# Reordering the prologue of an attention and MLP kernel: loads, transposes, column-tiled projections, and a halved last tile

## The chip, the cores and the metric

The kernel runs on one core of one Trainium2 chip. The metric is the device time of one execution in microseconds (us), the median over several runs. The profile shows one execution, whose span is about 1.8 us shorter than its measured time.

## The reference

`x` has 2048 tokens of 1024 channels. It is normalised, goes through attention with 32 heads of 32 channels, and in parallel, normalised once more, through an MLP of 3584 channels; the two are multiplied and added to `x`.

```python
xn = _layernorm(x, axis=-1)
s = attention(xn, wqkv, wo)                       # softmax(q k' / sqrt(32)) v, then @ wo
y = _layernorm(xn, axis=-1)
h = _gelu(y @ w1 + b1)
g = _silu(h @ w2 + b2)
return x + s * g
```

## The kernel before

The program is a list of operations with declared reads and writes; a small scheduler derives the semaphore waits from them. Attention is cut into 512 units (8 head groups, 8 query blocks, 8 key blocks): scores on TensorE, exponential on ScalarE, product with the values on TensorE. From unit 7 on, each unit also carries a "filler", a piece of projection, MLP or output product, so that TensorE and ScalarE are both full. Units 0 to 7 are the prologue: eight pairs of token tiles (128 tokens each) are loaded, normalised, transposed and projected to keys (K), queries (Q) and values (V), one pair per unit.

```python
load_x(0); load_x(1)
load_wq(0, (1,))              # weights of K, 512 KB
load_x(2); load_x(3)
load_wq(0, (0, 2))            # weights of Q and V
for tb in range(4, NT):
    load_x(tb)
...
def pair_kq(p):               # V likewise: 16 matmuls per pair
    for which, nm, dst, off in ((1, "KT", KT, 0), (0, "QT", QT, 256)):
        def f(e, which=which, off=off):
            for dc in range(DC):          # DC = 8
                ins = e.matmul(bank(bk, off, off + 256), lhsT=wq[:, which, dc, 0:128],
                               rhs=xnT[:, dc, t0:t0 + 256], start=dc == 0, stop=dc == DC - 1, ...)
...
def mm4(e, outs, lhs, rhs, start, stop):  # four column tiles of 32, used by every filler
    for j in range(4):
        ins = e.matmul(outs(j), lhsT=lhs(j), rhs=rhs, start=start, stop=stop,
                       tile_position=(0, 32 * j), ...)
```

Transposes of tiles 0 to 5 run on TensorE, those of tiles 6 to 15 as DMA transposes. The rule in the scheduler: a DMA names a semaphore, and waits for the previous DMA on the same one.

```python
prev = self.dlast.get(dma)
if prev is not None:
    deps.append(prev)
```

The softmax here doesn't subtract the row's maximum and nothing guards it: scores larger than these inputs give would overflow.

## Time and profile before

| | before |
|---|---|
| time, median (lowest to highest of 3) | 1092.49 us (1092.04 to 1092.57) |
| span of the profiled execution (itself 1093.07 us, 0.58 above the median) | 1091.3 us |
| scores of unit 7, of unit 8 (start) | 49.30, 51.89 us |
| TensorE matmuls in 30.35 to 49.30 | 226 |
| last full-width VectorE add of the last tile (start) | 1087.32 us |
| last store issued | 1088.89 us |

Three marks are used throughout. The start of the scores of unit 8 ends the prologue. The last full-width VectorE add marks the end of the long middle part. What follows it is the tail.

### The profile page before, as it was taken

Reading aid. Unit: us, or ns where it says so; the run is one execution under the profiler, and the core shown is the slowest. Engines: PE = TensorE matmul, PEld = TensorE weight load, DVE = VectorE, ACT = ScalarE, POOL = GpSimd, SP = SyncE. Lnnn points to the kernel's source line nnn. Section 1 sums busy time; section 2 is a strip of 40 time slices with the busy share of each in tenths; the row PEclk is TensorE's granted clock in tenths of the full one; section 3 lists DMA queues with packets and bytes.
Section 4 is the critical chain, followed back from the end, with each engine's and each line's share of the span. In section 5 each row is a group of like instructions: output and inputs, shape, how many; then the busy total and the mean of one; then the engine's idle time right before and its main releaser. Section 6 shows DMA issues by size and latency. Waiting matters only on the chain.

```text
span 1091.3 us, 61755 instructions
## 1 busy us (share of the span) xinstructions
PE 1079.6 (99%) x29129; PEld 701.6 (64%) x29129; DVE 628.0 (58%) x1395; ACT 1041.3 (95%) x1192; POOL 22.4 (2%) x68
## 2 busy tenths in 40 slices
PE   8999999999999999999999999999999999999998
PEld 5766666666666666666666666666666666666665
DVE  7388752477732576642377743378733387625556
ACT  5799998999999999999999999999999999999994
POOL 3400000000000000000000000000000000000000
PEclk9999999999999999999999999999999999999999
DMA  7844456323374123445333264423254343694443
GB/s 240 166 138 138 120 156 164 103 78 109 100 172 120 50 80 109 116 106 143 86 108 95 72 146 132 126 80 109 81 129 121 91 119 109 184 233 95 117 91 104
DMA packets 209192, 131.92 MB, mean 121 GB/s; under 512 B 52522, under 2 KB 199978, under 8 KB 208938
## 3 DMA queue, kind: packets, MB, share of 16 engines
q1 hardware_dynamic: 208938, 127.97, 43.7%
q8 instruction: 228, 3.74, 1.5%
q14 instruction: 26, 0.21, 0.1%
HBM read 104.87 MB, written 12.06 MB: 107 GB/s over the span
## 4 chain that ended last, share of the span: by engine, by line
PE 54%; ACT 43%; DVE 2%; DMA 1%; SPq 0%; issue 0%
ACT P L852 39%; PE ps L386 33%; PE ps L840 9%; PE ps L869 5%; PE ps L872 5%; ACT u L556 4%; DVE stats L322 1%; PE ps L674 1%; PE ps L690 1%; DMA OT<-in_A_x_dram 1%; DMA xnT<-hT 1%; DVE hT L350 0%; ACT thz L600 0%; SPq L284 0%; SPq L274 0%
## 5 line engine op out<-in xcount | busy, mean ns | idle before, releaser
L852 ACT ACTIVATE P<-ps 128x1024 bf16<-128x1024 f32 x1024 | 968.5, 1082 | 10.5 <-PE ps L840 5.8
L872 PE MATMUL ps<-P,ones 128*32 128x256 bf16 x4096 | 256.8, 273 | 0.0
L869 PE MATMUL ps<-P,VP 128*32 128x256 bf16 x4096 | 256.6, 273 | 0.0
L386 PE MATMUL ps<-hT,war 128*32 128x352 bf16 (+1 forms) x5376 | 225.5, 309 | 0.0
L386 PE MATMUL ps<-yTc,war 128*32 128x352 bf16 (+1 forms) x5376 | 225.5, 309 | 0.0
L840 PE MATMUL ps<-QT,KT 32*128 32x256 bf16 x4096 | 203.4, 273 | 3.2 <-ACT P L852 0.6
L386 PEld LDWEIGHTS ps<-hT,war 128*32 128x32 bf16 x5376 | 127.8, 96 | 74.2 <-issue 25.5
L386 PEld LDWEIGHTS ps<-yTc,war 128*32 128x32 bf16 x5376 | 127.4, 96 | 74.3 <-DVE xb L539 19.0
L840 PEld LDWEIGHTS ps<-QT,KT 32*128 32x128 bf16 x4096 | 60.7, 92 | 115.6 <-issue 61.3
L596 DVE TENSOR_SCALAR zh<-ps,b2h 128x352 f32<-128x352 f32 (+1 forms) x48 | 27.4, 572 | 183.1 <-PE ps L386 183.1
L539 DVE TENSOR_SCALAR xb<-ps,b1T 128x352 f32<-128x352 f32 (+1 forms) x168 | 96.2, 572 | 48.2 <-PE ps L386 43.3
L562 DVE SCALAR_TENSOR_TENSOR hT<-u,xb 128x352 bf16<-128x352 f32 (+1 forms) x168 | 84.3, 509 | 68.3 <-ACT u L556 68.2
L869 PEld LDWEIGHTS ps<-P,VP 128*32 128x32 bf16 x4096 | 109.6, 97 | 20.7 <-issue 1.5
L872 PEld LDWEIGHTS ps<-P,ones 128*32 128x32 bf16 x4096 | 109.4, 97 | 18.6
L386 PE MATMUL ps<-xnT,wq 128*32 128x352 bf16 (+1 forms) x2688 | 112.7, 309 | 0.0
L386 PEld LDWEIGHTS ps<-xnT,wq 128*32 128x32 bf16 x2688 | 63.8, 96 | 37.0 <-DVE xb L539 8.9
L549 DVE SCALAR_TENSOR_TENSOR u<-u,xb 128x352 f32<-128x352 f32 (+1 forms) x168 | 82.4, 508 | 1.9
L545 DVE TENSOR_TENSOR u<-xb 128x352 f32<-128x352 f32 (+1 forms) x168 | 82.3, 506 | 0.7
L556 ACT ACTIVATE u<-u 128x704 f32<-128x704 f32 (+1 forms) x84 | 71.6, 857 | 0.0
L386 PE MATMUL ps<-xnT,OT 128*32 128x352 bf16 (+1 forms) x1536 | 63.1, 309 | 1.0 <-issue 0.8
L386 PEld LDWEIGHTS ps<-xnT,OT 128*32 128x32 bf16 x1536 | 37.3, 96 | 21.1 <-DVE wq L657 7.7
L386 PE MATMUL ps<-wq,xnT 128*32 128x256 bf16 x1536 | 50.8, 274 | 0.0
(52 smaller groups left out, 477.3 us busy)
## 6 DMA issues: line engine op xcount, KB each, us to landing
war<-in_B_w_dram SPq DMA_DIRECT2D x336, 256.0 KB, 3.5
wq<-in_A_wqkv_dram SPq DMA_DIRECT2D x36, 128.0 KB, 2.6
OT<-in_A_x_dram SPq DMA_DIRECT2D x16, 256.0 KB, 5.0
xnT<-in_A_x_dram SPq DMA_DIRECT2D x16, 256.0 KB, 3.2
out_dram<-wq SPq DMA_DIRECT2D x16, 256.0 KB, 2.0
y_scratch<-OT SPq DMA_DIRECT2D x14, 256.0 KB, 2.8
gT_scratch<-gst SPq DMA_DIRECT2D x32, 88.0 KB, 3.2
xnT<-in_A_wo_dram SPq DMA_DIRECT2D x8, 256.0 KB, 4.1
```

The costliest lines, as they stand in the source:

```text
L322: op("vector", lambda e, c=c: e.bn_stats(stats[:, tb, c, :], xt[:, c * 512:(c + 1) * 512]), r=[("xst", tb)], w=[("st", tb, c)], c=677.0)
L386: ins = e.matmul(outs(j), lhsT=lhs(j), rhs=rhs, start=start, stop=stop, tile_position=(0, 32 * j), skip_group_check=True)
L539: x0 = op("vector", lambda e: e.tensor_scalar(xb[:, 0:n], bank(bk, 0, n), b1T[:, f:f + 1], None, op0=ALU.add), r=[("b", bk), "b1"], w=[kx] ...
L545: x = op("vector", lambda e: e.tensor_tensor(ub[:, 0:n], xb[:, 0:n], xb[:, 0:n], op=ALU.mult), r=[kx], w=[ku], c=151 + 1.042 * n)
L549: x = op("vector", lambda e: e.scalar_tensor_tensor(ub[:, 0:n], ub[:, 0:n], 1.0 / 0.044715, xb[:, 0:n], op0=ALU.add, op1=ALU.mult), r=[kx, ...
L556: x = op("scalar", lambda e: e.activation(ut[:, :, 0:n], ut[:, :, 0:n], ACT.Tanh, scale=0.7978845608028654 * 0.044715), r=kus, w=kus, c=48 ...
L562: op("vector", lambda e: e.scalar_tensor_tensor(hT[:, fq, 0:n], ut[:, i, 0:n], 1.0, xq[:, 0:n], op0=ALU.add, op1=ALU.mult), r=[kus[i], kq] ...
L596: x0 = op("vector", lambda e: e.tensor_scalar(zh[:, 0:n], bank(bk, 0, n), 0.25, b2h[:, nb:nb + 1], op0=ALU.mult, op1=ALU.add), r=[("b", bk ...
L840: ins = e.matmul(bank(bks[j], kh * 256, (kh + 1) * 256), lhsT=KT[i2][32 * j:32 * j + 32, k0:k0 + 128], rhs=QT[i2][32 * j:32 * j + 32, qb * ...
L852: op("scalar", lambda e, p=p, sl=sl: e.activation(pb[:, 2 * p:2 * p + 2, :, :].rearrange("p a b q -> p (a b q)"), ps[:, sl * 1024:(sl + 1) ...
L869: e.matmul(bankq(ACC, j, 0, QW), lhsT=VP[vp][:, kb, vo + 32 * j:vo + 32 * j + 32], rhs=pb[:, j, kh, :], start=first, stop=False, tile_posi ...
L872: ins = e.matmul(bankq(ACC, j, QW, 2 * QW), lhsT=ones[:, 0:32], rhs=pb[:, j, kh, :], start=False, stop=last, tile_position=(0, 32 * j), sk ...
```

## The change

It intends to start the attention sooner. Tiles 4 and 5 load ahead of the value weights, so that VectorE doesn't wait; transposes of the next pair go ahead of the values; from pair 2 on, projections use the four-way column tiling of everything around them (one matmul over 128 columns becomes four of 32 columns each), which spares TensorE a change of tiling mode; the seam between prologue and steady state uses other banks; and the last output tile is finished in two halves, 704 and 320 columns wide. The diff also moves the epsilon add of tiles 0 and 1 to VectorE and drops five warm-up matmuls. The core of the diff:

```diff
-        load_wq(0, (0, 2))
-        for tb in range(4, NT):
+        load_wq(0, (0,))
+        load_x(4)
+        load_x(5)
+        load_wq(0, (2,))
+        for tb in range(6, NT):
...
-            op("gpsimd", ... tensor_scalar(L(0), mv[:, lo:hi, 1], EPS, ...))
+            op("vector" if hi <= 2 else "gpsimd", ... tensor_scalar(L(0), mv[:, lo:hi, 1], EPS, ...))
...
+                        if p >= 2:
+                            ins = mm4(e, lambda j: bankq(bk, j, off, off + 256),
+                                      lambda j: wq[:, which, dc, 32 * j:32 * j + 32], xnT[:, dc, t0:t0 + 256], ...)
+                            continue            # likewise for the values
...
-        for k, after in ((18, None), (1, 0), (5, 1)):      # warm-up matmuls
+        for k, after in ((13, None), (1, 0), (5, 1)):
...
-            return p if u < NP else (2 * u + p) % 3        # banks of the scores
+            return p if u < NP else (2 * u + p + 1) % 3
...
-            if LAG <= u < NP:
+            if LAG <= u < NP - 1:                          # unit 6's product moves behind the first filler
                 pv_unit(u - LAG)
...
-                if k == len(ncol) - 1:
-                    op("sync", ... dma_start(out2[...rows, :], obf[o3]), ..., dma=f"os{o3}")
+                if k in ((2,) if tb < NT - 1 else (1, 3)):
+                    lo, hi = (0, D) if tb < NT - 1 else (0, 704) if k == 1 else (704, D)
+                    op("sync", ... dma_start(out2[...rows, lo:hi], obf[o3][:, lo:hi]), ..., dma=f"os{o3}")
```

More of the change, by code (lines that the diff above doesn't have):

```diff
@@ L13 @@
 PLAN = """
-q a a a a q a a q a q v a a a q q a a v v a a a v v a a a a a a a q v a a q v a a a a q q q w2 q v w4 w4 w2 w2 q v w2 q w4 w4 a a a a a q q a v q a a a a a v v q a q a a v a q q a v a a a a v a q a q q v a a a a a a w2 v w4 q w4 w2 w4 w4 w4 w3 a v a q a a v q q q a q v a q a a v a q q a a q a q a v q a a a v v a a a a q q q v a q a a q a q a q v a v a q a w3 w4 q q q w4 w3 v w4 w3 w4 w3 q v a v v a a a v a a a v q a a a a q v a a v v q a a v q a a v q a a a q a q a a a v q a a a q a w3 w4 w4 w4 w4 q v q q w4 w4 w3 a a a v a q a a a q a q a q a a a v a a a a q a a v a a v q a q a a q a a q q q v v a v a a w2 q v w4 w4 q w5 w3 q q w4 w4 w4 a a a a a q a a q a a a a a a q a q a a a q a a a q q a a q a q a a a a a w2 w4 w3 w4 w3 o o o o o o o o o o w4 o o o o o o o o o o o o w4 o o w4 o o o o o o o o o o o o o o o o o o o o o o . o o .
+q a a a a q a a q a q v a a a q q a a v v a a a v v a a a a a a a q v a a q v a a a a q q q w2 q v w4 w4 w2 w2 q v w2 q w4 w4 a a a a a q q a v q a a a a a v v q a q a a v a q q a v a a a a v a q a q q v a a a a a a w2 v w4 q w4 w2 w4 w4 w4 w3 a v a q a a v q q q a q v a q a a v a q q a a q a q a v q a a a v v a a a a q q q v a q a a q a q a q v a v a q a w3 w4 q q q w4 w3 v w4 w3 w4 w3 q v a v v a a a v a a a v q a a a a q v a a v v q a a v q a a v q a a a q a q a a a v q a a a q a w3 w4 w4 w4 w4 q v q q w4 w4 w3 a a a v a q a a a q a q a q a a a v a a a a q a a v a a v q a q a a q a a q q q v v a v a a w2 q v w4 w4 q w5 w3 q q w4 w4 w4 a a a a a q a a q a a a a a a q a q a a a q a a a q q a a q a q a a a a a w2 w4 w3 w4 w3 o o o o o o o o o o w4 o o o o o o o o o o o o w4 o o w4 o o o o o o o o o o o o o o o o o o o o o o . o o . o
 """
@@ L328, in rstd @@
             L = lambda k: lnp[:, k, lo:hi]
-            op("gpsimd", lambda e: e.tensor_scalar(L(0), mv[:, lo:hi, 1], EPS, None, op0=ALU.add), r=[("mv", t) for t in range(lo, hi)],
-               w=[("l0", t) for t in range(lo, hi)])
+            op("vector" if hi <= 2 else "gpsimd", lambda e: e.tensor_scalar(L(0), mv[:, lo:hi, 1], EPS, None, op0=ALU.add),
+               r=[("mv", t) for t in range(lo, hi)], w=[("l0", t) for t in range(lo, hi)], c=169.0)
             op("gpsimd", lambda e: e.tensor_tensor(L(2), L(0), mhalf[:, 0:hi - lo], op=ALU.pow), r=[("l0", t) for t in range(lo, hi)] + ["mhalf"],
@@ L629, in load_gres, with cols @@
                r=[("gT", nb, c) for nb in range(DC) for c in cs], w=[("gres", i4)], dma=f"rg{i4}", c=380, after=[tail["xfree"]] + pace)
+        def cols(tb):
+            return ncol if tb < NT - 1 else ncol[:2] + [(704, 160), (864, 160)]
         def wo_item(tb, k):
-            n0, n = ncol[k]
+            n0, n = cols(tb)[k]
             i4 = tb % NTB
@@ L660, in fin @@
                    r=[("ofin", f2), ("xres", i4)], w=[("obf", o3, k)], c=151 + 1.042 * n)
-                if k == len(ncol) - 1:
-                    op("sync", lambda e: e.dma_start(out2[tb * 128:(tb + 1) * 128, :], obf[o3]),
-                       r=[("obf", o3, q) for q in range(len(ncol))], w=[("out", tb)], dma=f"os{o3}", c=256)
+                if k in ((2,) if tb < NT - 1 else (1, 3)):
+                    lo, hi = (0, D) if tb < NT - 1 else (0, 704) if k == 1 else (704, D)
+                    op("sync", lambda e: e.dma_start(out2[tb * 128:(tb + 1) * 128, lo:hi], obf[o3][:, lo:hi]),
+                       r=[("obf", o3, q) for q in range(len(cols(tb))) if lo <= cols(tb)[q][0] < hi], w=[("out", tb, lo)], dma=f"os{o3}", c=256)
             return Item([lambda bk, hc=hc: step(hc, bk) for hc in range(HG)], fin, pre=pre)
@@ L673, in f @@
                     for dc in range(DC):
+                        if p >= 2:
+                            ins = mm4(e, lambda j: bankq(bk, j, off, off + 256), lambda j: wq[:, which, dc, 32 * j:32 * j + 32],
+                                      xnT[:, dc, t0:t0 + 256], dc == 0, dc == DC - 1)
+                            continue
                         ins = e.matmul(bank(bk, off, off + 256), lhsT=wq[:, which, dc, 0:128], rhs=xnT[:, dc, t0:t0 + 256],
@@ L677, in pair_kq @@
                 op("tensor", f, r=[("wq", which, s) for s in range(4)] + [("xnT", 2 * p), ("xnT", 2 * p + 1)],
-                   w=[("b", bk, off)] + ([("b", bk)] if off == 0 else []), c=("full", 8, 256))
+                   w=[("b", bk, off)] + ([("b", bk)] if off == 0 else []), c=("col" if p >= 2 else "full", 8, 256))
             for nm, dst, off in (("KT", KT, 0), ("QT", QT, 256)):
@@ L689, in f @@
                     for dc in range(DC):
+                        if p >= 2:
+                            ins = mm4(e, lambda j: bankq(bk, j, 256 * i, 256 * i + 256), lambda j: xnT[:, dc, t0 + 32 * j:t0 + 32 * j + 32],
+                                      wq[:, 2, dc, :], dc == 0, dc == DC - 1)
+                            continue
                         ins = e.matmul(bank(bk, 256 * i, 256 * i + 256), lhsT=xnT[:, dc, t0:t0 + 128], rhs=wq[:, 2, dc, :],
@@ L692, in f @@
                 return ins
-            op("tensor", f, r=[("wq", 2, s) for s in range(4)] + [("xnT", 2 * p), ("xnT", 2 * p + 1)], w=[("b", bk)], c=("full", 16, 256))
+            op("tensor", f, r=[("wq", 2, s) for s in range(4)] + [("xnT", 2 * p), ("xnT", 2 * p + 1)], w=[("b", bk)], c=("col" if p >= 2 else "full", 16, 256))
             op("scalar", lambda e: e.activation(VP[0][:, 2 * p:2 * p + 2, :].rearrange("p a n -> p (a n)"), bank(bk), ACT.Copy),
@@ L746, in pro_unit @@
             pair_kq(p)
-            if p == 0:
-                pair_v(p)
             for t in range(2 * p + 2, 2 * p + 4):
@@ L751, in pro_unit @@
                     transp(t)
-            if p:
-                pair_v(p)
+            pair_v(p)
             if p == 3 + 2:
@@ L773, in bass_recurrent_scan__mha_block__mixer_channel_mlp__prompt_kernel @@
         w2s = [w2_item(c, nb) for c in range(NCH) for nb in range(DC)]
-        wos = [wo_item(tb, k) for tb in range(NT) for k in range(len(ncol))]
+        wos = [wo_item(tb, k) for tb in range(NT) for k in range(len(cols(tb)))]
         qks, vs = [], []
@@ L816, in bass_recurrent_scan__mha_block__mixer_channel_mlp__prompt_kernel @@
                 elif kind == "o":
-                    tb = NT - len(wos) // len(ncol) - (len(wos) % len(ncol) > 0)
+                    tb = min((3 * NT + 1 - len(wos)) // 3, NT - 1)
                     assert t + DU >= (HG - 1) * UPH + NKP * (tb // 2 + 1) + 4 and q_end
@@ L968, in bass_recurrent_scan__mha_block__mixer_channel_mlp__prompt_kernel @@
                         soon(NPC + 16, ("gres", t), load_gres, t)
-            if NP <= u < NU + LAG:
+            if NP - 1 <= u < NU + LAG:
                 pv_unit(u - LAG)
@@ L974, in bass_recurrent_scan__mha_block__mixer_channel_mlp__prompt_kernel @@
                 hurry(lambda: not dq and not act_tasks)
-        op("sync", None, r=[("out", t) for t in range(NT)])
+        op("sync", None, r=[("out", t, 0) for t in range(NT)] + [("out", NT - 1, 704)])
         pg.finalize()
```

## The prediction

> **What bounds the kernel now.** I read the page first: the busy table, then the shares of the chain that ended last.
>
> ```profile
> PE 1079.6 (99%) x29129; PEld 701.6 (64%) x29129; DVE 628.0 (58%) x1395; ACT 1041.3 (95%) x1192; POOL 22.4 (2%) x68
> ...
> PE 54%; ACT 43%; DVE 2%; DMA 1%; SPq 0%; issue 0%
> ```
>
> TensorE and ScalarE share the path for nearly the whole span. The compiled order of the changed kernel, set against the old one, shows that from the ninth attention unit to the last output tile no engine's sequence changes. So roughly 1,035 us in the middle can only be moved in time, not shortened, and the case is decided in the first 52 us and the last 4 us. The stretches view gives the room: TensorE is busy 8.90 of the first 10.66 us, 4.97 of the next 6.21, all of 16.87 to 30.35, 18.10 of 18.95 up to 49.30, and 6.25 of the 6.70 up to 56.0. Next I read the timeline of those stretches (start, length, engine, line, operation, then the idle time before it and its releaser).
>
> ```profile
> 12.22 1.29 DVE L322 BATCH_NORM_STATS2 stats<-OT 128x6 f32<-128x512 bf16 x2 [1.07 <-DMA OT<-in_A_x_dram]
> 12.40 1.91 PE L690 MATMUL ps<-wq,xnT 128*128 128x256 bf16 x16
> 13.67 0.95 DVE L350 TENSOR_SCALAR hT<-OT,mv,lnp 128x1024 bf16<-128x1024 bf16 x2
> 14.22 1.08 PE L377 MATMUL ps<-ident,hT 128*128 128x128 bf16 x16
> 16.87 1.92 PE L674 MATMUL ps<-xnT,wq 128*128 128x256 bf16 x16 [1.24 <-ACT xnT L380]
> 26.54 0.28 PE L872 MATMUL ps<-P,ones 128*32 128x256 bf16 x4
> 26.75 1.92 PE L674 MATMUL ps<-xnT,wq 128*128 128x256 bf16 x16
> 32.15 1.92 PE L674 MATMUL ps<-xnT,wq 128*128 128x256 bf16 x16 [0.85 <-DMA xnT<-hT]
> 51.89 0.40 PE L840 MATMUL ps<-QT,KT 32*128 32x256 bf16 x8 [0.45 <-ACT P L852]
> ```
>
> VectorE's statistics of token tile 4 wait 1.07 us for its load, and the normalisation of tiles 2 and 3 (13.67) stands behind them in the queue; TensorE's transposes (14.22) and pair 1's projections (16.87) hang on that. Pair 4 waits 0.85 us for DMA transposes. At 51.89 the first scores unit after the prologue waits 0.45 us for an exponential that holds its banks.
>
> The end of the chain, in order of time (start, length, what), then the SyncE timeline and the DMA issues (size, us to landing) of the last store:
>
> ```profile
> 1087.32 0.52 DVE wq L659
> ...
> 1087.85 0.50 DVE wq L657
> ...
> 1088.37 0.49 DVE wq L659
> ```
>
> ```profile
> 1088.89 0.33 SPq L662 DMA_DIRECT2D out_dram<-wq  x1
> ```
>
> ```profile
> out_dram<-wq SPq DMA_DIRECT2D x1, 256.0 KB, 2.0
> ```
>
> Two VectorE operations of about 0.49 us follow the last matmul; the store, issued at 1088.89, lands about 1090.9, and the span ends 0.4 us later.
>
> **What the Trainium skill says.** "TensorEngine Tiling (Array Packing)", Key Properties: changing the tiling mode drains the engine. The trace agrees: groups of the same mode start 0.11 us apart, but from the column-tiled group at 26.54 to the full-array group at 26.75 it takes 0.21, so a switch costs about 0.10. The same page, Restrictions, says column tiling disables Fast Weight Load. That could make the column-tiled projections slower; the trace says it does not at this width: later column-tiled value items (32 matmuls, 128x256) start at 72.97 and the next group at 73.85, 0.88 us for eight rounds, where sixteen full ones take 1.75. "DMA: Bandwidth & Descriptors", Anatomy of one DMA, puts a fixed cost of about 2 us on each transfer, most of it the write receipt; the last store's 2.0 us agrees. (The page states it for the other descriptor path.) "TensorE: Matmul & The Clock Gate", Part 1, gives 426.7 ns for a cold 512-column matmul; the warm-up matmuls here start 0.43 us apart until 6.85 us, as it says.
>
> **The change part by part.**
>
> Load order. The 512 KB value weights go behind tiles 4 and 5. The query weights landed at 3.77 + 6.1 = 9.87, the value weights at 4.25 + 7.2 = 11.45 (DMA issues), so 512 KB take 1.58 us and a 256 KB tile 0.79: I estimate tile 4 at 10.7 instead of 12.2, tile 5 at 11.5, the value weights at 13.0.
>
> Epsilon add of tiles 0 and 1 on VectorE. It spares a hop over GpSimd (0.23 to 0.41 us) but adds a small VectorE operation, some 0.2 us, twice. Normalising tile 0 is later (6.85 for 6.41), tile 1 earlier (7.6 for 7.77), and everything behind 0.18 earlier. Statistics of tile 3 end at 10.97; those of tile 4 start at once, 11.04 instead of 12.22: VectorE gains **1.18 us** and, since it was busy without a gap to 35 us, keeps it. With 13 warm-up matmuls (1.38 + 13 x 0.427 = 6.93) the first transposes start near 7.4, not 7.93, and pair 0's projections at 10.1, not 10.66. That gain is off the path: after them TensorE waits for tile 2.
>
> Transposes ahead of values. Transposes of tiles 2 and 3: 14.22 - 1.18 = 13.04 to 14.05. Then the values, which formerly filled the wait: 1.75 plus a switch 0.10, to 15.90. Scores of unit 0 start there (0.67 later than the old 15.23), taking 0.33; pair 1 starts at 16.23, gain 0.64. But ScalarE had the old first exponential at 16.70, and the new one follows the value copy, 15.95 + 0.6 = 16.55: only 0.15 earlier, ending 18.50. The copies of pair 1's keys and queries follow to 19.16, and the value bank is theirs; values of pair 1 start at 19.2 against 19.54. So at scores of unit 1 the gain is **0.34**.
>
> Column-tiled projections. Same array time, one switch less per pair: 0.10 to 0.11 for pairs 2 to 7, but one more around the bias transpose in pair 5. Pairs 2 and 3 start 0.45 and 0.56 earlier. Pair 4 would be ready at 32.15 - 0.92 (the stall, 31.23 to 32.15) - 0.67 = 30.56, but tile 9's transpose, moved by VectorE's 1.18, lands at 32.10 - 1.18 = 30.92. So it starts near 30.97: gain **1.18**, of which the shorter stall is the largest part. Pairs 5 to 7 add 0.33 less 0.11: **1.40** at the end of the values of pair 7.
>
> Bank rotation and the order at the seam (in the diff, not in its title). Scores of unit 8 use banks freed by the first half of unit 7's exponential, not the second, and the product with values moves behind the filler. Unit 8 starts 0.33 + 1.19 + 0.55 = 2.07 us after unit 7 instead of 51.89 - 49.30 = 2.59; the exponential follows without a gap: **0.5** on both engines. Prologue total: 1.9.
>
> Last tile in halves. The remainder becomes two 160-column items. At about 1 ns per column (0.52 against 0.49 for 352 against 320) the last two VectorE operations shrink from 0.99 to some 0.65. But both stores of the last tile use one semaphore, and the program makes a transfer wait for the previous one on its semaphore: the compiled order lists the 320-column store as waiting for the landing of the 704-column store. In old times: first store at 1087.89, landing 2.0 later at 1089.89; second issued 1089.94, landing with 1.9 to 2.0 at 1091.9, instead of 1090.9. That is **0.95 lost**, not 0.35 gained. The matmuls of the halves are hidden beneath the wait.
>
> Sum: 1.9 - 0.95 = 0.95, and up to 1.35 if tile 9's transpose no longer stalls. I take 1.1: 1092.5 - 1.1 = 1091.4.
>
> **The rivals.**
> First, the store wait is cheaper than two full transfers, or absent. For: 176 KB and 80 KB are smaller than 256 KB. Against: the wait stands in the compiled order, and other stores of the tail took 2.0 to 2.6. Without it the gain would be 1.9 + 0.35: 1090.2.
> Second, the pair 4 stall goes or grows. Tile 9's transpose took 5.5 us where tile 8's took 2.7, and the stretches view shows only 17 GB/s in 28.5 to 29.5, so it is a hold-up, not volume. Without it 0.4 more: 1091.0; if it stays at its old time, pair 4 gains nothing and the total is 0.72 - 0.95, a loss of 0.2: 1092.7.
> Third, ScalarE becomes the bound of the prologue. In pairs 2 to 4 it has about 4.1 us of work (7.43 busy in 8.08, two periods of 4.48) and the period becomes 4.37: close, but enough. If it binds, 0.3 of the switches is lost: 1091.7.
> Fourth, fewer warm-up matmuls leave the array cold. The gap is about 0.5 us; if the clock fell, pair 0 would last 1.75 us longer, to 13.6, and transposes would slip by 0.6: 1092.0.
>
> **Range and chances.** The parts that could fail are each 0.3 to 1.3 us; runs before spread by 0.53. The best case of the first two rivals together is 1089.8, the worst near 1093. I take 1090.0 to 1092.8. The 2% line is 21.8 us away and the whole prologue idle time is under 6 us: within 2% at 0.98, 0.01 to either side.
>
> **What would show it right or wrong.** In the changed profile: statistics of tile 4 near 11.0 without a DMA wait; pair 1's projections near 16.2; pair 4 near 31.0, still with a DMA wait of some 0.4; unit 7 to unit 8 2.07 us apart, with no wait on the exponential; and at the end two stores, the second issued about 2 us after the first, the span ending about 0.95 later after the last full-width VectorE pair. Wrong would be: column-tiled projections over 1.8 us per pair half, value weights arriving after 14 us, or the second store leaving at once.

## The result, and the profile after

The changed kernel took 1096.46 us (median of 4 runs, 1095.46 to 1096.77), against 1092.53 (1092.04 to 1092.9) for the kernel before. The ratio is 1.0035, with a 95% interval of 1.0017 to 1.0052. Ratios are the mean time of one kernel's runs over that of the other's of the same rounds, so they differ slightly from the ratio of the medians. The time is within 2%, as forecast, but outside the range and on the wrong side: some 3.8 us slower instead of 1.1 faster. The profiled executions, 1093.07 and 1096.31 us, differ by 3.2.

The page of the changed kernel, busy table and shares of the chain:

```profile
PE 1079.2 (99%) x29732; PEld 704.2 (64%) x29732; DVE 628.4 (57%) x1399; ACT 1041.5 (95%) x1192; POOL 21.7 (2%) x66
...
PE 56%; ACT 40%; DVE 2%; DMA 1%; issue 1%; POOL 0%
```

The busy times of matmuls, VectorE and ScalarE are the same to 0.4 us, while TensorE has 603 more matmuls and "issue", time in which an engine waits for nothing that the profile shows, now has 1% of the chain. The timeline of the changed kernel at the places of the prediction:

```profile
11.12 1.23 DVE L325 BATCH_NORM_STATS2 stats<-OT 128x6 f32<-128x512 bf16 x2
...
16.16 1.92 PE L685 MATMUL ps<-xnT,wq 128*128 128x256 bf16 x16
...
34.60 0.40 PE L852 MATMUL ps<-QT,KT 32*128 32x256 bf16 x8
...
51.27 0.40 PE L852 MATMUL ps<-QT,KT 32*128 32x256 bf16 x8
...
53.34 0.40 PE L852 MATMUL ps<-QT,KT 32*128 32x256 bf16 x8
```

The early steps came as forecast: statistics of tile 4 at 11.12 without a DMA wait, pair 1 at 16.16. The seam also works: units 7 and 8 are 2.07 us apart. But unit 7 itself starts at 51.27, 1.97 us later than before. The scores of units 4 and 7 in the kernel before:

```profile
35.74 0.40 PE L840 MATMUL ps<-QT,KT 32*128 32x256 bf16 x8
...
49.30 0.40 PE L840 MATMUL ps<-QT,KT 32*128 32x256 bf16 x8
```

At unit 4 (34.60) the changed kernel was still 1.14 us ahead, so the loss lies in pairs 5 to 7: they took 16.67 us instead of 13.56. The chain of the changed kernel in order of time (start, length, what) shows why:

```profile
35.89 3.06 PE ps L389 x113
38.95 0.97 issue
39.92 0.62 PE ps L389 x15
...
41.54 2.40 PE ps L389 x87
43.94 0.45 issue
44.38 1.36 PE ps L389 x41
...
46.62 1.74 PE ps L389 x63
48.37 0.94 issue
49.31 2.03 PE ps L389 x65
```

TensorE stops three times in the middle of a projection, 2.36 us in all, with no semaphore to wait for. This idle time understates the loss, since the profile draws a matmul's modelled end some 0.27 us after its start: from the start of one matmul to that of the next the three stops take 1.25, 0.72 and 1.22 us, where a round of four usually follows the last by 0.11. A fourth one, at 35.28, takes 0.35 and hardly shows as idle. Between the first and the second stop it runs 15 + 1 + 8 + 16 + 87 = 127 matmuls (the left-out lines are the bias transpose, scores and products), between the second and the third 41 + 8 + 16 + 63 = 128. Every matmul has its weight load, an instruction of its own (29,732 of each on the page), so 128 matmuls are 256 instructions. The trace's instruction packets, those of the page's "instruction" queue, are 16,384 bytes each, and there are 5 more than before. The queue's lines of both pages (packets, MB, share), before first:

```profile
q8 instruction: 228, 3.74, 1.5%
```

```profile
q8 instruction: 233, 3.82, 1.5%
```

The stretches view of both kernels (length, then TensorE matmuls busy and count, weight loads, VectorE, ScalarE, GpSimd, clock, DMA share, GB/s), before first:

```profile
30.35:49.30 18.95, 18.10 (x226) 14.09 (x226) 5.12 (x12) 13.63 (x23) 11.06 (x34) 1.00 1.01 199
```

```profile
30.35:49.30 18.95, 16.53 (x544) 13.81 (x536) 4.01 (x9) 12.85 (x21) 10.56 (x33) 1.00 1.14 170
```

The instructions of the stretch more than doubled, the busy time fell by 1.57 us, and the mean DMA share was 1.14 (the shares add up transfers in flight, so they can pass 1). The Trainium skill, "Runtime: NRT & Kernel Launch", Instruction fetch mechanics, says that a sequencer refills its instructions in blocks of 16 KiB, 256 instructions, over a DMA queue of its own. This trace agrees: packets have that size and the stops are that far apart. The page also says that the cost is mostly hidden; here it is not. The waits view names all such stops, before and after (in total, times, longest):

```profile
PE ps L386 <- issue: 0.8, 1, 0.8
```

```profile
PE ps L389 <- issue: 3.4, 6, 1.0
PE ps L881 <- issue: 0.5, 1, 0.5
```

Before, there was one:

```profile
979.23 0.48 PE L386 MATMUL ps<-xnT,OT 128*32 128x352 bf16 x8 [0.82 <-issue]
```

The number of TensorE instructions ahead of a stop, counted in the trace with weight loads and semaphore instructions, is 1473, 1729 and 1986 in the prologue of the changed kernel and 52,418 at 979 us of the kernel before. Divided by 256 these leave 193, 193, 194 and 194; the fourth, small stop stands at 1217, which leaves 193. At the three prologue stops an instruction packet had started at 36.81, 41.90 and 47.04 us, and ended 1.3 to 1.5 us before TensorE went on.

The tail, on SyncE and in the DMA issues of the changed kernel:

```profile
1090.16 0.33 SPq L669 DMA_DIRECT2D out_dram<-wq  x1
```

```profile
1092.46 0.33 SPq L669 DMA_DIRECT2D out_dram<-wq  x1
```

```profile
out_dram<-wq SPq DMA_DIRECT2D x1, 176.0 KB, 2.2
```

```profile
out_dram<-wq SPq DMA_DIRECT2D x1, 80.0 KB, 1.6
```

The last full-width VectorE add and the last VectorE operation:

```profile
1089.61 0.53 DVE L665 TENSOR_TENSOR wq<-wq,xnT 128x352 bf16<-128x352 f32 x1
...
1090.99 0.32 DVE L665 TENSOR_TENSOR wq<-wq,xnT 128x160 bf16<-128x160 f32 x1
```

The last VectorE operation ended at 1090.99 + 0.32 = 1091.31; the second store left only at 1092.46, when the first had landed.

The account of the two profiled spans, in the traces 1094.46 - 1091.28 = 3.18 us: unit 8 is 53.34 - 51.89 = 1.45 later; the last full-width add 1089.61 - 1087.32 = 2.29 later, so the middle lost 0.84; the tail after that add takes 4.85 instead of 3.96, 0.89 more.

### The profile page after: what moved, and what is told of

It is laid out like the page before. It is cut to its first block, busy times and chain, and to the rows that moved or that the text cites. A ratio compares the mean times of both kernels' runs of the same rounds, so it can differ in the third digit from the quotient of the medians.

```text
span 1094.5 us, 62966 instructions
## 1 busy us (share of the span) xinstructions
PE 1079.2 (99%) x29732; PEld 704.2 (64%) x29732; DVE 628.4 (57%) x1399; ACT 1041.5 (95%) x1192; POOL 21.7 (2%) x66
## 4 chain that ended last, share of the span: by engine, by line
PE 56%; ACT 40%; DVE 2%; DMA 1%; issue 1%; POOL 0%
ACT P L864 36%; PE ps L389 36%; PE ps L852 9%; PE ps L881 6%; PE ps L884 6%; ACT u L559 3%; DVE stats L325 1%; DMA xnT<-hT 0%; DMA war<-in_B_w_dram 0%; ACT thz L603 0%; DVE hT L353 0%; DMA OT<-in_A_x_dram 0%; DVE mv L327 0%; DVE wq L663 0%; DVE zh L599 0%
## 5 line engine op out<-in xcount | busy, mean ns | idle before, releaser
L389 PE MATMUL ps<-xnT,wq 128*32 128x352 bf16 (+2 forms) x3072 | 124.6, 305 | 1.4 <-issue 0.9
L389 PEld LDWEIGHTS ps<-xnT,wq 128*32 128x32 bf16 x3072 | 74.2, 96 | 39.3 <-DVE xb L542 9.1
L389 PE MATMUL ps<-wq,xnT 128*32 128x256 bf16 x1920 | 62.9, 274 | 1.4 <-issue 1.4
L389 PE MATMUL ps<-xnT,OT 128*32 128x352 bf16 (+2 forms) x1568 | 63.1, 306 | 0.3 <-DVE wq L663 0.2
L389 PEld LDWEIGHTS ps<-wq,xnT 128*32 128x32 bf16 x1920 | 47.0, 96 | 12.8 <-DVE xb L542 5.3
```

## The experiments

Theory: TensorE's instruction blocks come late, because a pair of tiles with column-tiled projections needs 304 instructions (64 + 64 + 8 + 16 matmuls, each with a load) in 4.4 us where 112 sufficed, and DMA is busy; the tail loses by a shared semaphore. Rivals: column tiling itself disturbs TensorE; the new load order and the moved transposes are at fault; the tail is slow because of small packets. All kernels gave correct results. Runs of one call share a chip and the runs of the kernel before: e1 to e4, then a0, e7, e8 and e9, then e10 to e12. "Against before" is the difference of the means. The kernel before spread from 1091.47 to 1094.81 us, so single differences under 1 us say little, and the traces carry the argument. All these differences are far under 2%, within which runs count here as the same.

| run | median us | against before | ratio, 95% interval | stops of kind "issue" in 20 to 56 us | unit 8 at |
|---|---|---|---|---|---|
| e1 full projections | 1091.76 | -1.34 | 0.9987 (0.9972 to 1.0002) | none | 51.15 |
| e2 two columns | 1091.14 | -1.96 | 0.9981 (0.9966 to 0.9996) | none | 49.84 |
| e3 own semaphore | 1092.54 | -0.45 | 0.9994 (0.9978 to 1.0011) | 3, 1.3 us | 51.67 |
| e4 shifted blocks | 1095.92 | +2.93 | 1.0026 (1.0006 to 1.0046) | 5, 3.4 us | 54.25 |
| a0 after again | 1094.66 | +1.23 | 1.0009 (0.9994 to 1.0024) | 2, 1.1 us | 51.79 |
| e7 two columns, own semaphore | 1091.85 | -1.46 | 0.9983 (0.9966 to 1.0) | none | 50.18 |
| e8 seam only | 1091.79 | -0.55 | 0.9993 (0.9976 to 1.0009) | none | 51.41 |
| e9 columns only | 1094.91 | +2.12 | 1.0017 (1.0002 to 1.0032) | 3, 1.5 us | 53.62 |
| e10 early weights | 1093.57 | +0.53 | 1.0004 (0.9989 to 1.0019) | 1, 0.7 us | 51.67 |
| e11 two, own, early | 1092.45 | -0.70 | 0.9992 (0.9979 to 1.0006) | none | 50.02 |
| e12 full, own, early | 1092.23 | -1.16 | 0.9988 (0.9976 to 1.0001) | none | 50.16 |

### e1: projections back on the full array

```diff
-                        if p >= 2:
+                        if p >= NP:        # never: both projections
```

> The changed kernel with the projections of pairs 2 to 7 back on the full array, all else kept. Theory (TensorE runs out of instructions: its idle stretches inside groups, released by nothing, end 127, 128 and 128 matmuls apart, that is 256 instructions of load and matmul, and an instruction packet of 16 KB ends 1.3 to 1.5 us before each): a quarter of the projections' instructions, so no idle of kind 'issue' before 56 us; scores of unit 8 start near 50.7 instead of 53.34 (some 3.1 us of stalls gone, 0.55 of mode switches back); total 1093.1 to 1093.9. Rival (the loss comes from the load order, the moved transposes or the seam): scores of unit 8 stay near 53.3 and the total near 1096.5.

Measured: no stop in the prologue, 1091.76 us, below the expected 1093.1 to 1093.9. The stretches view of this run:

```profile
30.35:49.30 18.95, 18.29 (x234) 14.15 (x233) 4.54 (x10) 13.66 (x24) 11.00 (x34) 1.00 1.03 195
```

With 234 matmuls TensorE is busy 18.29 us again; the missing 0.66 is the old wait of pair 4 for a DMA transpose. Unit 8 starts at 51.15, 0.74 before the kernel before, later than the expected 50.7: VectorE waited 0.59 us for tile 2 in this execution (statistics of tile 4 at 11.64, not 11.12), and pair 4 waited. The rival that blames load order and transposes falls.

### e2: two column tiles of 64 instead of four of 32

```diff
-                            ins = mm4(e, lambda j: bankq(...), lambda j: wq[:, which, dc, 32 * j:32 * j + 32], ...
+                            ins = mm2(e, lambda j: bankh(...), lambda j: wq[:, which, dc, 64 * j:64 * j + 64], ...
```

> The changed kernel with the projections of pairs 2 to 7 in two column tiles of 64 instead of four of 32: column tiling stays, instructions halve (176 instead of 304 per pair with scores and products, so a block of 256 lasts about 6.3 us instead of 3.7). Theory of instruction supply: no idle inside groups before 56 us, or under 0.5 us in all; scores of unit 8 near 50.2; total 1093.0 to 1093.8. Rival (column tiling as such, or its weight loads, disturbs TensorE while the DMA transposes run): stalls of about the same 2.4 us remain, total near 1096.5.

Measured: no stop in the prologue, unit 8 at 49.84, 1091.14 us. The time is lower than expected, since I had taken only the prologue stops off the changed kernel and here the middle lost little as well (one stop of 0.43 us, at 515.58). The stretches view:

```profile
30.35:49.30 18.95, 18.95 (x381) 16.12 (x373) 3.87 (x9) 14.37 (x26) 10.42 (x33) 1.00 0.89 180
```

Column tiling as such doesn't stop TensorE: it has no gap here. The trace's instruction packets ended at least 3.6 us ahead of each block border up to 50 us, against 1.3 to 1.5 at the three stops of the changed kernel. There was a side result. From unit to unit this kernel takes 4.49 us (25.18 to 29.67), like the full array (4.48, 25.87 to 30.35 before), where the four-way tiling takes 4.37 (20.83 to 25.20 after). So the switch is spared only where the tiles have the same width.

### e3: a semaphore of its own for the last store

```diff
-                       ..., w=[("out", tb, lo)], dma=f"os{o3}", c=256)
+                       ..., w=[("out", tb, lo)], dma=f"os{o3}" if lo == 0 else "os3", c=256)
```

> The changed kernel with a semaphore of its own for the 320-column store of the last tile. Theory (the second store waits for the landing of the first): the second store is issued about 0.1 us after the last VectorE operation, some 1.1 us earlier against that operation than in the changed kernel; the span ends about 3.0 us after the last full-width VectorE operation instead of 4.4; total 1.0 to 1.4 below the changed kernel, 1095.1 to 1095.5. Rival (the end is set by the smaller packets of the halves, or by the final wait): under 0.4 us.

Measured, on VectorE and SyncE in this run:

```profile
1087.09 0.53 DVE L665 TENSOR_TENSOR wq<-wq,xnT 128x352 bf16<-128x352 f32 x1
...
1088.48 0.32 DVE L665 TENSOR_TENSOR wq<-wq,xnT 128x160 bf16<-128x160 f32 x1
```

```profile
1088.83 0.33 SPq L669 DMA_DIRECT2D out_dram<-wq  x1
```

The second store leaves at 1088.83, 0.03 us after the last VectorE operation (1088.48 + 0.32 = 1088.80) instead of 1.15 after it. The tail from the last full-width add (1087.09) to the end of the span (1090.83) takes 3.74 us, against 4.85 in the changed kernel and 3.96 before: 1.11 recovered, in the expected range, and the halved tile is worth 0.22 once its wait is gone. The other traces agree: the tail takes 3.73 to 3.86 us in the four kernels with the own semaphore (e3, e7, e11, e12), 4.43 to 5.07 in the six where the halves share one, and 3.96 in the three with the old last tile. The rival of small packets falls: the 80 KB store landed in 1.6 us. The whole kernel gained 3.9 us against the changed kernel's first runs, three times what was expected. That isn't the tail alone: the stops of the prologue were smaller (1.3 us for 2.4), at the same counts 1473, 1729 and 1986, and the middle was 0.84 shorter. This asked for a0.

### e4: block borders moved against the program

```diff
-                ins = e.matmul(bank(0), lhsT=ident[:], rhs=cold, ...)             # 512 columns
+                if k == 13:                                                        # the first 13
+                    for _ in range(4):
+                        ins = e.matmul(bank(0, 0, 128), lhsT=ident[:], rhs=ident[:], ...)
+                    continue
```

> The changed kernel with its first 13 warm-up matmuls of 512 columns issued as 52 of 128 columns: the same array time, 78 more TensorE instructions ahead of everything. Theory of instruction supply: idle stretches of kind 'issue' again end where the count of TensorE instructions is 193 or 194 over a multiple of 256, as in all seven such stalls of the two kernels so far, so at other matmuls of the program (39 matmuls earlier in it); the total stays within 1 us of the changed kernel. Rival (the stall belongs to certain matmuls of the projections, by a conflict with a DMA transpose): the stalls stay at the same matmuls, 78 instructions later in the count.

Measured: 1095.92 us (two runs), within 1 us of the changed kernel. Five stops in the prologue, after 961, 1218, 1473, 1729 and 1986 TensorE instructions, and two in the middle, at 341.60 and 963.91 us after 18,113 and 52,673; the last three of the prologue are the very counts of the changed kernel, though each stands 39 matmuls earlier in the program. The remainders by 256 are again 193 or 194. Two of the stops in the timeline:

```profile
44.30 0.62 PE L389 MATMUL ps<-xnT,wq 128*32 128x256 bf16 x16 [0.36 <-issue]
...
49.22 1.27 PE L389 MATMUL ps<-xnT,wq 128*32 128x256 bf16 x40 [1.02 <-issue]
```

In the changed kernel the second stop (44.38) stood in the values of pair 6 and the third before the last matmul of pair 7's keys and queries. Here the one at 44.30 stands in the keys and queries of pair 6, the other before the 25th of the 64 matmuls of pair 7's, instead of the 64th. A stop belongs to an instruction count, not to a matmul: the rival of a conflict with certain matmuls falls.

### a0: the changed kernel once more

No edit.

> The changed kernel once more, unaltered. The kernel with its own semaphore for the last store came out 3.9 us below the changed kernel, where the tail explains 1.2: its prologue stalls were smaller (three of 0.42, 0.45 and 0.39 us against 0.97, 0.45 and 0.94) although its prologue is the same program. If the size of a stall varies with the execution (how long the instruction packet waits among the other transfers), this run shows stalls at the same counts of TensorE instructions (1473, 1729, 1986) of another size, and the total lies between 1093.5 and 1096.8. If the sizes belong to the kernel, they are again near 2.4 us in all and the total is 1096.0 to 1096.8.

Measured, on another chip than e1 to e4: 1094.66 us (1092.09 to 1095.21), two stops in the prologue of 0.45 and 0.67 us, at counts 1729 and 1986, and two in the middle of 0.63 and 0.82. The size of a stop varies with the execution, and with it whether one shows; the counts at which stops stand don't. So the 3.8 us of the first comparison belong partly to those executions or to their chip, which these runs can't tell apart; the same program came out 1.2 us over the kernel before, which is not separable from it (0.9994 to 1.0024).

### e9: the column tiling alone

```diff
 # the kernel before, and in pair_kq and pair_v:
+                        if p >= 2:
+                            ins = mm4(e, ...)      # as in the change
+                            continue
```

> The kernel before with the projections of pairs 2 to 7 in four column tiles of 32 alone; load order, transposes, seam and last tile as before. Theory of instruction supply: stalls of kind 'issue' inside the projections of pairs 4 to 7, at counts 193 or 194 over a multiple of 256, 1 to 3 us in all, less 0.55 of saved switches: total 0.5 to 2.5 above before. Rival (the stalls need the earlier DMA transposes of the new load order): no stall, total 0.5 below before.

Measured: 1094.91 us, 2.1 above before. The timeline of this run:

```profile
40.10 0.73 PE L386 MATMUL ps<-wq,xnT 128*32 128x256 bf16 x19 [0.64 <-issue]
...
44.57 1.48 PE L386 MATMUL ps<-wq,xnT 128*32 128x256 bf16 x45 [0.46 <-issue]
...
48.95 0.40 PE L386 MATMUL ps<-xnT,wq 128*32 128x256 bf16 x6 [0.39 <-issue]
```

The counts are 1474, 1730 and 1985. Unit 7 starts at 51.03 instead of 49.30. This one part, alone in the old kernel, makes the stops, without the new load order. Pair 3 also waited 0.69 us for a DMA transpose.

### e8: the seam alone

```diff
-            return p if u < NP else (2 * u + p) % 3
+            return p if u < NP else (2 * u + p + 1) % 3
-            if LAG <= u < NP:
+            if LAG <= u < NP - 1:
-            if NP <= u < NU + LAG:
+            if NP - 1 <= u < NU + LAG:
```

> The kernel before with the seam alone: bank rotation moved by one, and the product of unit 6 behind the first filler. Theory: scores of unit 8 follow those of unit 7 by 2.07 us instead of 2.59 with no wait for the exponential, total 0.5 below before; rival (the half microsecond is lost again to ScalarE or to the DMA loads behind it): same total, or the wait appears within the next three units.

Measured in the timeline of this run:

```profile
49.33 0.40 PE L840 MATMUL ps<-QT,KT 32*128 32x256 bf16 x8
...
51.41 0.40 PE L840 MATMUL ps<-QT,KT 32*128 32x256 bf16 x8
```

Units 7 and 8 are 2.08 us apart and the wait is gone, as expected, nor does it come back in the next three units. The time, 0.55 us below before on the means, fits but isn't separable from it (four runs, 1091.2 to 1094.71).

### e7: both causes removed

The edits of e2 and e3 together.

> Two column tiles of 64 for the projections, and the last store with its own semaphore: both causes removed. Theory: the sum of the two, 1091.1 less 1.2, so 1089.7 to 1090.3, and the last store's end 3.2 us after the last full-width VectorE operation; no prologue stall inside a group. Rival (the two gains overlap, or the last run with its own semaphore was only lucky): 1091 or more.

Measured: 1091.85 us, above the expected 1089.7 to 1090.3 and where the rival had put it (1091 or more); one of the four runs took 1089.65. The prologue is free of stops with unit 8 at 50.18. But the middle had stops of 0.29, 0.39 and 0.55 us of kind "issue" (at 421.60, 961.42 and 971.16) and one wait of 0.57 for MLP weights. What the prologue and the tail gain, the middle can take away in one execution.

### e10, e11, e12: the weight loads moved out of the crowd

```diff
-            if 2 <= p < 2 + 4:
-                load_sub(0, p - 2)
+            if p == 0:
+                for q in range(4):
+                    load_sub(0, q)
```

e10 is the changed kernel with this edit alone; e11 adds those of e2 and e3, e12 those of e1 and e3.

> The changed kernel with the four 256 KB loads of the first MLP weights issued right behind the token tiles, near 14 us, where the DMA engines fall idle after 16 us, instead of one by one between 31 and 45 us among the DMA transposes. Instructions of TensorE are unchanged. If the instruction packets are late because they wait among the other transfers, a thinner queue from 31 to 45 us makes the stalls at counts 1473, 1729 and 1986 smaller: under 0.8 us in all (1.1 to 2.4 in the changed kernel's two traces), scores of unit 8 near 50.5, total 0.8 to 1.8 below the changed kernel. Rival (the packets are late for a reason of their own, such as the time from request to arrival): stalls of 1.1 to 2.4 us as before. A third outcome: the early loads delay the last token tiles and the first DMA transposes, and a wait for a tile takes the place.

> The version meant to beat both: the changed kernel with two column tiles of 64, an own semaphore for the last store, and the early weight loads. Prologue without a stall inside groups, scores of unit 8 at 49.5 to 50.2; end of the span 3.2 us after the last full-width VectorE operation; total 2.0 to 3.0 below before. Against it: stalls of the middle at block borders between 960 and 980 us, which moved with every build so far (0 to 1.7 us), can take back 1 us; then 1.0 to 2.0 below before.

> The same with the projections on the full array as in the kernel before. By the count of switches it loses 0.55 us in the prologue against two column tiles (six switches of 0.11, less one); if it is as fast or faster, the switches were not worth the change at all. Total 1.4 to 2.4 below before.

Measured for e10: one stop of 0.70 us, at count 1473, none at 1729 and 1986; unit 8 at 51.67. The stops fell under the 0.8 us set, yet a0 has 1.1 us without the edit, and single executions differ by as much. Nor did the edit thin the traffic as it was meant to: from 31 to 45 us the DMA share of this run is 1.18, against 1.13 in the changed kernel and 1.08 in a0. So this doesn't settle why the packets are late. The third outcome came too: pair 3 waited 0.94 us for its DMA transpose. The middle had 1.10, 0.21 and 0.66 us of stops; the total, 0.5 above before, is not separable from it.

e11 and e12 came out 0.7 and 1.2 us below before, less than the 2.0 to 3.0 and 1.4 to 2.4 expected. e11's prologue is clean (unit 8 at 50.02) and its middle has stops of 0.33, 0.75 and 0.45 us. e12 came out no slower than e11, and their units 8 start at 50.16 and 50.02, so these runs show no gain from two column tiles; the four-way form was not run with both other edits.

A version that beats both kernels: e2 is the only one whose interval against the kernel before excludes 1 (0.9966 to 0.9996), and it is 0.2% faster; one such interval among eleven runs is weak evidence. It lacks e3's tail, and e7, which has both, measured no better; the four of e1, e2, e7 and e12 can't be ordered by these runs.

## Why the prediction was wrong

**What bounds the kernel.** That TensorE and ScalarE hold the path was right. The claim that the middle "can only be moved in time, not shortened" left out that the middle has stops of its own, which differ from execution to execution. Between the two profiles they went from one of 0.82 us to 0.54, 0.53, 0.28 and 0.21, and the middle lost 0.84 us. That the change did this, by shifting every later block border by some 600 matmuls, is not shown. From unit 8 to the last full-width add the same program took 1036.26, 1036.55 (a0) and 1035.42 us (e3, whose edit comes later), the last no longer than the 1035.43 of the kernel before. Over all traces this stretch took 1034.1 to 1035.4 us in the four kernels with full-array projections (before, e1, e8, e12) and 1035.4 to 1036.6 in the six with four column tiles, which leans that way. The waits view of the kernel before already held that one "issue" line, and the prediction passed over it.

**Load order, epsilon, warm-up, transposes.** Right. Statistics of tile 4 began at 11.12 (11.04 predicted), pair 1 at 16.16 (16.23), unit 1 gained 0.56 us (0.34 predicted, too little).

**Column-tiled projections: the step that failed.** It read "Same array time, one switch less per pair", and summed to a gain of 1.40 us at the end of pair 7. The array time and the switch were right (4.37 us from unit 1 to unit 2 instead of 4.48). That pair 4 started at 31.00, 30.97 predicted, is luck: the wait that was to set it had gone, and one of 0.47 before pair 3 stood in its place. The step priced array time alone. It left out that four column tiles are four times the projections' instructions, 304 instead of 112 per pair with scores and products, so that a block of 256 is used up in 3.7 us (4.37 x 256 / 304) instead of 10.2 (4.48 x 256 / 112), while each block has to arrive by DMA. Unit 7 was 1.97 us late instead of 1.40 early. Nearly all of this difference of 3.37 lies where the stops stand: pairs 5 to 7 were to take 13.34 us (13.56 less the 0.22 that the prediction adds for them) and took 16.67, 3.33 more. e9 shows this part alone produces the stops, e1 and e2 that with a quarter or half of the projections' instructions they vanish from the prologue, and e4 that they stand at instruction counts.

**Pair 4's stall.** Predicted to remain with 0.3 to 0.4 us; it was gone, and pair 3 waited 0.47 us for a DMA transpose instead. The hold-up of DMA transposes wanders between executions: pair 4 waits in e1, pair 3 in a0, e9 and e10, neither in e2.

**The seam.** Right: 2.07 us after, and 2.08 with the seam alone (e8).

**The last tile.** Right, in mechanism and size: 0.89 us lost in this pair of profiles (0.95 predicted), the second store 2.30 us behind the first, and 1.11 recovered with its own semaphore (e3).

**The rivals.** None of the four was it. The warm-up and ScalarE rivals didn't occur: the transposes at 7.43 ran at the same pace as before, and without stops the units followed one another in 4.37 us.

With the column step at what it measured, the forecast would have been about 1094.9: 1.45 late at unit 8 and 0.89 in the tail, 2.3 us over before. The rest is mainly the middle's 0.84.

How narrow the margin is can be estimated from the traces. Over all 2,999 instruction packets of the 13 traces the median packet starts 0.6 us after the block ahead of it comes into use and takes 1.1 us, and at the stops TensorE went on 1.2 to 1.6 us after a packet's end. That adds up to an estimated 3.1 us, of the 3.7 that a block lasts with four column tiles, the 6.5 with two (4.49 x 256 / 176) and the 10.2 with the full array. At the three prologue stops the packet started 1.5 to 2.7 us after.

What stays open is why a packet is late. It goes with busy DMA engines: where the other queues kept them busy for under 30% of the time around the border (from 1 us before to 0.5 us after it), the median start was 0.4 us after the border, where for over 90%, 1.1 us, with one in ten later than 2.3. This is a coincidence counted in the traces and not a test; the run that was to thin the traffic (e10) didn't.

## What to carry to other kernels

Price a tiling by its instructions as well as by its array time. Here TensorE ran dry in the prologue where a block of 256 instructions lasted 3.7 us and DMA was full, and not where it lasted 6.5 or 10.2; single stops in the middle came with blocks of 4.9 to 5.9 us, the stop included. The profile calls such a stop "issue" inside a group. Count the instructions between such stops before looking for a semaphore. And when a transfer is split to overlap its halves, check that the second doesn't wait for the first one's completion.

## What the Trainium skill lacked or had wrong

- "Runtime: NRT & Kernel Launch", Instruction fetch mechanics, calls the refill hidden by the pace of issue. Here TensorE stood 0.2 to 1.1 us at block borders, in 12 of the 13 traces (all but e8); in the three prologue stops of the changed kernel it went on 1.3 to 1.5 us after the packet's end.
- The same section gives TensorE 2048 instructions of buffer, and elsewhere two blocks. The trace fits the second: no packet up to 56 us in these traces started more than 1.8 us before the block ahead of it came into use.
- "TensorEngine Tiling (Array Packing)" doesn't say that column tiling multiplies the instructions (112 to 304 per pair here), nor what a switch of mode costs (about 0.11 us, also from 32-wide to 64-wide tiles: 4.49 us per unit against 4.37).
- "DMA: Bandwidth & Descriptors", Anatomy of one DMA, has its fixed 2 us for the GpSimd path; on SyncE's queue the output stores of 80 to 256 KB landed in 1.6 to 4.2 us, with a median of 2.0 before and 2.1 after.
